# A gated linear attention with a convolution stage: exp and ln table loaded first, sine table moved between two groups of exponentials, and a new order of the whole program

## The chip, the cores and the metric

The kernel runs on one core of a Trainium2 chip. The metric is the device time of one execution in microseconds (us); lower is better. A core has five engines with a queue each that works strictly in its order: PE (TensorE, matrix products; its weight loads are listed as PEld), DVE (VectorE), ACT (ScalarE), POOL (GpSimd) and SP (SyncE, which here only issues DMAs). They wait for one another through semaphores.

## The reference

Two stages, float32 in and out: a recurrent attention (4 batches, 8 heads, 768 steps, 48 columns) and a gate with a circular convolution over the 768 steps.

```
for t in range(S):                      # state: (B, H, D, D)
    cur   = outer(u * k_t, v_t)
    y_t   = r_t @ (state + cur)
    state = w_t * state + outer(k_t, v_t)

x    = y as (B, S, H*D)
proj = x @ w_proj                       # split into x1, x2, x3
conv = irfft(rfft(x2, axis=1) * rfft(filter_fft, axis=0))
out  = (x1 * conv * x3) @ w_out
```

## The kernel before

The sequence is cut into 24 chunks of 128 steps, six to a batch. The matrices of the Fourier transform (the tiles F and mi) are made on the chip: DVE and POOL compute angles (`ang`, `ia`), ACT takes their sine (`sin0` to `sin2` and `is`, line 1520). Sine needs one table of ACT, exp and ln need another. `trig` (line 1514) loads the first, `table` (line 1564) the second; a copy works under either.

First stage, for chunk i (loads and some steps are for a group gi: chunk 0, chunk 1, then pairs):

- SP loads w, k, r, v (`lw`, `lk`, `lr`, `lv`, line 1307, 192 KB each) into rings of 3 (w) and 4 groups.
- ACT: `ln` of w (line 1313). PE: `cs`, running sums of the logarithms by a triangular mask (lines 1341 to 1344). ACT: `ex`, their exponentials in PSUM (line 1347), and `ph`, the decay of a whole chunk (line 1354). DVE: `kq`, exponentials times k and r (line 1350).
- PE: `tr`, eight transposes of kq (line 1362); `qk` copies them out of PSUM (DVE or ACT); PE: `sc`, the scores (line 1374); `mt` and `mc` copy and mask them.
- POOL and DVE: `rk`, `ru`, `rh`, `cc`, `vb`, `vc`, the term with u. PE: `ki`, `kv`, and DVE `su` (line 1425), the state handed from chunk to chunk; PE: `yi`, `ys`, `y`, the output; `xn` copies it out, `yt` (PE) and `xT` transpose it.

Second stage, for batch b: PE products `xw` (line 1653), `p` and `q` (line 1616), the forward transform `f` (line 1505), the inverse `E` (line 1708), the output `o` (line 1772); between them copies (`cxw`, `cp`, `cq`, `cf`, `cE`, `co`), sums and products on DVE and POOL (`sd`, `u`, `p`, `aE`, `dE`, `yE`), and `so`, the stores (SP, line 1788). The filter's spectrum is made once: `filt` (load), `fsd`, `h`, `hc`, `hg`. `if0` to `if3` make mirrored parts of mi. `warm n b` issues n products of zeros on PE (line 1253) that no result needs.

All of this stands as a table of operations (`plan.op`) with what they read and write. The text ORDER, some thousand lines, gives the order: the queue of an engine is its operations in the order of that text. A line names the operation, its engine (P, A, D, G for POOL, S; a few further letters choose a form: M and N mask a whole chunk's scores on DVE or ACT, C masks them on POOL in one piece, Q is an inverse with folded halves at fewer columns, V and X ways to do `xn`, "-" nothing), for PE its PSUM bank, and at times another operation on DVE that a POOL operation is to wait for.

Of the kernel before, what the change touches and what calls it, by code (L numbers as in the profile page):

```python
# [215 lines left out]
yi3 P 0
ys3 P
y3 P
tr5 P 2
xn3 D  # L220
xa3 -
qk4 A
qk5 D
yt2 P 5
rk3 G
ru3 G
lr6 S
lr7 S
lk7 S
yt3 P 1  # L230
sc4 P 3
ph5 A
xT2 A
xw0.0 P 6
lk6 S
filt S
vb3 G xn3
mt4.0 D
mt4.1 D
xT3 A  # L240
xw0.2 P 1
if0 A
cxw0.2 A
mc4.0 -
mc4.1 -
sc5 P 3
# [41 lines left out]
lv7 S
xw0.4 P 2
kq7 D  # L290
cxw0.4 A
ph7 A
p0.0.1 P 0
kq6 D
ph6 A
cp0.0.1 A
sd0.0.0 D
p0.2.1 P 2
tr6 P 4
tr7 P 5  # L300
qk6 A
cp0.2.1 D
qk7 A
# [228 lines left out]
qk12 D
xT11 A
sc12 P 6
qk13 A
aE0.0.0 D
aE0.0.1 D
cE0.1 D
mt12.1 -
lv16 S  # L540
kv12 P 3
mt12.0 N
E0.2 Q 4
su12 D
ki13 P 3
kv13 P
sc13 P 6
lv17 S
dE0.0.0 -
lr17 S  # L550
aE0.1.0 D
aE0.1.1 D
lw19 S
lk19 S
su13 D
cE0.2 A
ln8 A
p1.0.1 P 0
dE0.0.1 -
aE0.2.0 D  # L560
aE0.2.1 D
dE0.1.0 -
mt13.0 M
cs14 P 2
mt13.1 -
cp1.0.1 A
cc7 D
xw1.4 P 4
ex14 A
cxw1.4 A  # L570
vb8 A
p1.2.1 P 7
q1.0.1 P 0
kq14 D
ru8 G aE0.1.0
rh8 G mt13.0
# [1294 lines left out]
```

## Time and profile before

| what | value |
|---|---|
| median of 3 runs | 155.47 us (155.39 to 160.37) |
| the profiled execution's own time | 154.99 us |
| its span | 153.3 us |
| busy: PE, DVE, ACT, POOL | 143.9, 138.8, 123.8, 94.5 us |
| warm-up products on PE | 109, with 16.0 us of the busy time |
| granted clock of TensorE | 0.996 |
| DMA moved | 26.23 MB, mean 171 GB/s |

The profile is of one execution. A row of its timeline gives start, duration, engine, line, operation, output and inputs, count, and in square brackets the idle time before it and what ended it. A window's row gives the busy time of each engine in a stretch of the span, the clock granted to PE, the busy share of the 16 DMA engines and the rate. PE's products are pipelined, so a row's duration is longer than the distance to the next.

### The profile page before, as it was taken

The numbers are of one execution on the slowest core, as the hardware profiler recorded it, in microseconds if no ns is written. First come the engines' busy times: TensorE is split into PE (matmuls) and PEld (weight loads), VectorE is DVE, ScalarE is ACT, GpSimd is POOL, SyncE is SP. The second block draws the span as 40 slices with busy tenths as digits, with TensorE's granted clock in tenths as the row PEclk, the third lists the DMA queues.
The fourth block names the chain that finished last, engine by engine and source line by source line (L and its number), as shares of the span: only waits on it lengthen the run. The fifth ranks groups of instructions, "written<-read, shape, count | busy, mean of one in ns | idle before, by whom it ended". The sixth has DMA issues, their size and how long they took to land.

```text
span 153.3 us, 4449 instructions
## 1 busy us (share of the span) xinstructions
PE 143.9 (94%) x1742; PEld 97.3 (63%) x1742; DVE 138.8 (91%) x259; ACT 123.8 (81%) x207; POOL 94.5 (62%) x97
## 2 busy tenths in 40 slices
PE   7989899999999999999999979999999999999980
PEld 5867676576657666666566747566676666755640
DVE  7959998987989999999999899989999999999950
ACT  5699997628989978898899969999999866876370
POOL 6827979734056564889867928896889540820310
PEclk9999999999999999999999999999999999999998
DMA  5999899999989999999899899998900000002956
GB/s 99 200 227 223 166 222 172 214 182 286 230 168 212 185 184 205 181 207 216 165 213 227 162 219 186 192 209 164 361 36 0 4 0 0 4 0 82 397 208 240
DMA packets 104118, 26.23 MB, mean 171 GB/s; under 512 B 100129, under 2 KB 102690, under 8 KB 104098
## 3 DMA queue, kind: packets, MB, share of 16 engines
q1 hardware_dynamic: 102498, 24.78, 73.6%
q0 software_dynamic: 1600, 1.18, 5.6%
q8 instruction: 13, 0.21, 0.6%
q14 instruction: 7, 0.06, 0.2%
HBM read 22.41 MB, written 4.72 MB: 177 GB/s over the span
## 4 chain that ended last, share of the span: by engine, by line
PE 55%; DVE 18%; ACT 11%; issue 6%; DMA 6%; POOL 1%; ACTq 1%; SPq 0%; DVEq 0%
PE banks L1505 10%; PE banks L1616 9%; PE banks L1653 7%; PE banks L1772 6%; PE banks L1708 5%; DVE kq L1350 5%; PE banks L1362 3%; DMA w<-in_w_dram 3%; ACT banks L1347 3%; PE banks L1374 3%; DMA out_dram<-o 2%; PE banks L1253 2%; ACT lg L1313 2%; PE banks L1452 2%; DVE U L1203 2%
## 5 line engine op out<-in xcount | busy, mean ns | idle before, releaser
L1616 PE MATMUL banks<-xT,wproj 128*128 128x384 bf16 x144 | 27.6, 326 | 0.1
L1203 POOL TENSOR_TENSOR rk<-kr 128x768 bf16<-128x768 f32 (+1 forms) x13 | 22.0, 1694 | 7.8 <-DVE xT L1209 3.7
L1350 DVE TENSOR_TENSOR kq<-banks,kr 128x768 bf16<-128x768 f32 x24 | 22.5, 949 | 2.2 <-ACT banks L1347 2.0
L1207 ACT ACTIVATE x<-banks 128x768 bf16<-128x768 f32 (+1 forms) x26 | 17.8, 706 | 6.1 <-PE banks L1616 4.0
L1395 POOL TENSOR_SCALAR_AFFINE_SELECT mt<-mt 128x512 bf16<-128x512 bf16 (+1 forms) x17 | 14.4, 853 | 10.0 <-DVE rk L1323 6.0
L1203 POOL TENSOR_TENSOR vc<-vb,cc 128x768 bf16<-128x768 bf16 x11 | 17.9, 1625 | 3.6 <-DVE cc L1326 2.2
L1347 ACT ACTIVATE banks<-banks 128x768 f32<-128x768 f32 x24 | 19.3, 809 | 0.5 <-PE banks L1344 0.4
L1616 PEld LDWEIGHTS <-wproj 128*128 128x128 bf16 x144 | 13.2, 97 | 8.0 <-issue 0.4
L1207 ACT ACTIVATE qk<-banks 128x1024 bf16<-128x1024 bf16 x17 | 17.4, 1028 | 0.4 <-PE banks L1362 0.3
L1390 DVE TENSOR_TENSOR mt<-banks,mask_excl 128x1024 bf16<-128x1024 f32 (+1 forms) x18 | 16.9, 950 | 0.7 <-PE banks L1452 0.6
L1253 PE MATMUL banks<-wt 128*128 128x256 bf16 x109 | 16.0, 300 | 1.1 <-DVE wt L1276 1.1
L1362 PE MATMUL banks<-ident,kq 128*128 128x128 bf16 x192 | 14.2, 219 | 0.6 <-DVE kq L1350 0.5
L1653 PE MATMUL banks<-wproj,xT 128*128 128x384 bf16 x72 | 13.5, 326 | 1.1 <-DVE xn L1464 1.1
L1505 PE MATMUL banks<-sd,F 128*128 128x384 bf16 (+1 forms) x96 | 13.4, 328 | 0.0
L1772 PE MATMUL banks<-wout,y 128*128 128x384 bf16 x72 | 13.3, 326 | 0.0
L1253 PEld LDWEIGHTS <-wt 128*128 128x128 bf16 x109 | 10.8, 107 | 4.0 <-DVE wt L1276 1.1
L1362 PEld LDWEIGHTS <-kq 128*128 128x128 bf16 x192 | 11.3, 97 | 2.1 <-DVE kq L1350 1.5
L1207 ACT ACTIVATE o<-banks 128x768 f32<-128x768 f32 (+1 forms) x13 | 9.8, 764 | 3.5 <-PE banks L1772 3.3
L1505 PEld LDWEIGHTS <-F 128*128 128x128 bf16 (+1 forms) x120 | 8.4, 103 | 5.9 <-issue 1.5
L1641 DVE TENSOR_TENSOR g<-banks,x 128x768 bf16<-128x768 f32 (+1 forms) x16 | 11.8, 751 | 0.0
L1313 ACT ACTIVATE lg<-w 128x768 bf16<-128x768 f32 (+1 forms) x13 | 10.3, 803 | 1.6 <-DMA w<-in_w_dram 1.5
L1207 ACT ACTIVATE mt<-banks 128x512 bf16<-128x512 f32 (+1 forms) x17 | 11.5, 704 | 0.0
(109 smaller groups left out, 331.7 us busy)
## 6 DMA issues: line engine op xcount, KB each, us to landing
w<-in_w_dram SPq DMA_DIRECT2D x24, 192.0 KB, 4.4
kr<-in_r_dram SPq DMA_DIRECT2D x24, 192.0 KB, 3.8
kr<-in_k_dram SPq DMA_DIRECT2D x24, 192.0 KB, 3.9
v<-in_v_dram SPq DMA_DIRECT2D x24, 192.0 KB, 3.8
out_dram<-o SPq DMA_DIRECT2D x11, 384.0 KB, 3.5
U<-in_moe_filter_fft_dram SPq DMA_DIRECT2D x1, 1152.0 KB, 7.8
wproj<-in_moe_w_proj_dram POOLq DMA_DIRECT2D x3, 288.0 KB, 5.2
out_dram<-o SPq DMA_DIRECT2D x2, 192.0 KB, 2.2
```

What stands on the lines that cost most here:

```text
L1203: return eng(e).tensor_mul(o, a, b)
L1207: return nc.scalar.activation(out=o, in_=a, func=AF.Copy)
L1253: nc.tensor.matmul(banks[:, at, 0:256], wt[:, 0:L], wt, start=True, stop=True)
L1347: op(f"ex{i}", [ACT], lambda e, bk: nc.scalar.activation(out=two(bk, f"cs{i}")[:, :, 0:C], in_=two(bk, f"cs{i}")[:, :, 0:C], func=AF.Exp), ...
L1350: op(f"kq{i}", [DVE], lambda e, bk: nc.vector.tensor_mul(kq[f][:, :, :, 0:D], two(bk, f"cs{i}")[:, :, 0:C].rearrange("p a (h d) -> p a h d ...
L1362: nc.tensor.transpose(p[:, HP * m + j, :], kq[f][:, m, 2 * j:2 * j + 2, :], ident)
L1390: return copy(ACT, o, x) if e in (ACT, ACT2) else nc.vector.tensor_mul(o, x, _mid(mask_excl, z - HP * a))
L1395: return nc.gpsimd.affine_select(out=o, in_=o, pattern=[[0, z - HP * a], [1, L]], compare_op=ALU.is_gt, fill=0.0, base=0, channel_multipli ...
L1505: nc.tensor.matmul(p[rows], F[:, ti, c0 + rows.start:c0 + rows.stop], x[q][:, ti, :], start=(ti == 0), stop=(ti == NT - 1),)
L1616: nc.tensor.matmul(p, wproj[:, cb, col0:col0 + L], xT[bx][:, cb, sl], start=(cb == 0), stop=(cb == CB - 1),)
L1653: nc.tensor.matmul(view(bk)[:, z], xT[bx][:, cb, (c0 + z) * L:(c0 + z + 1) * L], wproj[:, cb, C:2 * C], start=(cb == 0), stop=(cb == CB - 1),)
L1772: nc.tensor.matmul(view(bk)[:, z], yt_[:, z, :], wout[:, cb, :], start=(cb == 0), stop=(cb == CB - 1),)
```

## The change

The code changes in the keys that tables stand for. A third load, `first`, brings the exp and ln table in ahead of everything on ACT. `trig` and the sines now come after the exponentials of chunks 4 and 5, then `table` brings exp and ln back for `ln4` and the exponentials of chunks 6 and 7 (`ex7`, `ex6`). ORDER is another text throughout. The operations are the same but for what follows: one more table load; 90 warm-up products for 109 (16 at the start for 46); one inverse, E0.2, in the full form for the folded one, and for it two `dE` fewer; the output of chunk 18 begins with `yi` on PE; and many copies, masks and small products on another engine than before (`ur` and `ub` from DVE to ACT, `cxw0.0`, `cxw0.2`, `cp0.0.0` and `cp0.2.0` all on DVE, three of six `ia` from DVE to POOL, `mt` in whole pieces 16 times for 13 on ACT and DVE, among others).

The code:

```diff
@@ op "ur"
-    op("ur", [DVE, ACT], lambda e, bk: copy(e, u_r, u_f), r=["uf", "trig"], w=["ur"])
+    op("ur", [DVE, ACT], lambda e, bk: copy(e, u_r, u_f), r=["uf", "first"], w=["ur"])
@@ group
-           r=keys("w", sw) + ["table", "pads"], w=[f"lg.{f}"])
+           r=keys("w", sw) + ["exp", "pads"], w=[f"lg.{f}"])
-            e, vb[fv][:, 0:n], vl[sl][:, 0:n]), r=keys("v", sl) + ["trig"], w=[f"vb.{fv}"])
+            e, vb[fv][:, 0:n], vl[sl][:, 0:n]), r=keys("v", sl) + ["first"], w=[f"vb.{fv}"])
@@ first
-           w=[f"ex.{i}"], uses=[f"cs{i}"])
+           r=["exp"], w=[f"ex.{i}"], uses=[f"cs{i}"])
-           r=[f"kq.{f}"], w=[f"phi.{f}"], uses=[f"cs{i}"])
+           r=[f"kq.{f}", "exp"], w=[f"phi.{f}"], uses=[f"cs{i}"])
@@ early
+        op("first", [ACT], lambda e, bk: nc.scalar.preload_act_table_set("natural_log_exp_and_others"),
+           w=["first", "exp"])
-        op("trig", [ACT], lambda e, bk: nc.scalar.preload_act_table_set("trig_and_small"), w=["trig"])
+        op("trig", [ACT], lambda e, bk: nc.scalar.preload_act_table_set("trig_and_small"), w=["exp", "trig"])
         op("table", [ACT], lambda e, bk: nc.scalar.preload_act_table_set("natural_log_exp_and_others"),
-           r=[f"F.{ti}" for ti in range(NT)] + ["m0"], w=["table"])
+           w=["exp", "trig"])
```

Parts of ORDER, four stretches with lines left out between them:

```diff
-wz D
-warm 46 7
-lw2 S
-zeros D
-kz0 D
-kz2 D
-smalls D
-kz3 D
-lr0 S
-maps G
-imaps G kz3
-lk0 S
-ang1 D
-ang2 D
-ia0.0 G ang2
-ia0.1 G ang2
-kz1 G
-lw0 S
-ang0 D
-ia2.0 D
-ia2.1 D
-ia1.0 D
-ia1.1 D
-maskn G
-maske G
-maski G
-rk0 G ia1.1
-pads D
-lw1 S
-trig A
-sin1 A
-sin2 A
-sin0 A
-is A
-u S
-ur D
-signs D
-table A
-ln0 A
-lw3 S
-lr3 S
-um P 4
-warm 11 7
-ub D
-ru0 D
-rh0 G ub
-cc0 D
-ln2 A
-lk3 S
-lr1 S
-lk1 S
-lr2 S
-lk2 S
-cs0 P 3
-ex0 A
-ln1 A
-kq0 D
-cs3 P 6
-lv0 S
-warm 7 0
-cs1 P 1
-ex3 A
-ph0 A
-kq3 D
-lv1 S
-lw4 S
-lv2 S
-lw5 S
-ex1 A
-kq1 D
-tr0 P 0
-cs2 P 3
-qk0 A
+wz D
+warm 16 0
+pads D
+smalls D
+zeros D
+lw0 S
+first A
+ln0 A
+imaps G
+maske G smalls
+maps G smalls
+ang2 D
+ang1 D
+lw3 S
+lw2 S
+lr0 S
+lk0 S
+kz2 G
+maskn G
+cs0 P 4
+kz0 G
+ln2 A
+u S
+signs D
+maski G
+ia1.0 G
+ex0 A
+kq0 D
+ia2.0 D
+warm 9 1
+cs3 P 6
+kz3 G zeros
+cs2 P 2
+ur A
+warm 5 1
+um P 0
+rk0 G
+ub A
+lv0 S
+lw1 S
+lr3 S
+lk1 S
+tr0 P 1
+qk0 D
+ph0 A
+vb0 A
+ex3 A
+ln1 A
+ang0 D
+ru0 G ia2.0
+rh0 G kq0
+cc0 D
+kz1 D
+vc0 D
+warm 6 0
+sc0 P 0
+warm 2 4
+cs1 P 4
+mt0.1 -
+mt0.0 N
...
-ex4 A
-mc3.0 G
-lw6 S
-su2 D
-yt1 P 3
-ki3 P 2
-wproj0 G cc2
-kq4 D
-xT1 D
-kv3 P
-ph4 A
-ex5 A
-mc2.0 -
-warm 2 5
-yi2 P 4
-ys2 P
-if1 A
-tr4 P 3
-y2 P
-xn2 A
-su3 D
-kq5 D
-xa2 -
-yi3 P 0
-ys3 P
-y3 P
-tr5 P 2
-xn3 D
-xa3 -
-qk4 A
-qk5 D
-yt2 P 5
-rk3 G
-ru3 G
-lr6 S
-lr7 S
-lk7 S
-yt3 P 1
-sc4 P 3
-ph5 A
-xT2 A
-xw0.0 P 6
-lk6 S
-filt S
-vb3 G xn3
-mt4.0 D
-mt4.1 D
-xT3 A
-xw0.2 P 1
-if0 A
-cxw0.2 A
+ex4 A
+cs5 P 2
+xa1 -
+mc2.0 -
+yt1 P 1
+su2 D
+ki3 P 0
+kv3 P
+yi2 P 6
+ys2 P
+y2 P
+mc3.1 -
+xT1 A
+kq4 D
+tr4 P 1
+ex5 A
+ph4 A
+wproj0 G su2
+kq5 D
+su3 D
+xn2 A
+yi3 P 4
+ys3 P
+qk4 A
+y3 P
+rk3 G
+xn3 D
+warm 4 6
+tr5 P 6
+qk5 D
+xa2 -
+ph5 A
+yt2 P 2
+lw7 S
+xa3 -
+yt3 P 7
+xT3 D
+xT2 D
+ki4 P 5
+warm 4 1
+sc5 P 6
+trig A
+sin0 A
+sin2 A
+vb3 G xn3
+mt5.1 -
+mc5.1 -
+ia1.1 G xT2
+kv4 P
+sc4 P 3
+ia0.1 G xT2
+mt4.0 N
+ru3 D
+rh3 D
+cc3 D
+vc3 G cc3
+warm 7 1
+xw0.2 P 0
+is A
+mt5.0 M
+su4 D
+mt4.1 -
+xw0.0 P 2
+mc5.0 -
+mc4.0 C
+yi5 P 6
+cxw0.2 D
+yi4 P 4
+cxw0.0 D
+lk7 S
+sin1 A
+table A
+ln4 A
+lr7 S
+mc4.1 -
+ys5 P
+ys4 P
+y5 P
+xn5 D
+y4 P
+xn4 D
+p0.0.0 P 0
+lk6 S
+xa4 -
+xa5 -
+yt5 P 6
+p0.2.0 P 3
+lr6 S
+rk4 G xn5
+xT5 D
+yt4 P 2
+cs7 P 6
+cp0.0.0 D
+filt S
+cp0.2.0 D
+cs6 P 4
+xT4 A
+xw0.4 P 0
+ex7 A
+kq7 D
+lv7 S
+ex6 A
+kq6 D
+cxw0.4 A
+if3 A
+p0.0.1 P 2
+tr7 P 1
+ph7 A
+cp0.0.1 A
+tr6 P 6
+qk6 A
+qk7 A
+sd0.0.0 D
+ru4 D
+lw8 S
+lw9 S
+p0.2.1 P 0
+ph6 A
...
-yi14 - 4
-ys14 P
-y14 P
-qk16 D
-xn13 A
-mc15.1 -
-xa13 -
-yt13 P 2
-xT12 A
-dE0.2.1 D
-ki16 P 3
-kv16 P
-sc16 P 6
-xn14 V
-ex17 A
-kq17 D
-xT13 A
-xw2.0 P 4
+yi14 - 3
+ys14 P
+lr18 S
+lv18 S
+yt12 P 5
+xa13 -
+su15 D
+yt13 P 2
+xT12 A
+y14 P
+xn14 X
+mc15.1 -
+ki16 P 7
+kv16 P
+sc16 P 5
+lv19 S
+lr19 S
+ln10 A
+rk9 G mt15.1
+xT13 D
+kq17 D
+mc15.0 -
+ph17 A
+mt16.1 A
+dE0.2.0 -
+xa14 G
+xw2.0 P 3
...
-lv23 S
-q2.2.1 P 7
-su20 D
-cs22 P 4
-yi18 - 2
-ex22 A
-rh11 G kq21
-sd2.1.0 D
-cq2.2.1 D
-tr21 P 6
-y18 P
-ki21 P 7
-lr22 S
-q2.0.1 P 0
-xn18 X
-sd2.0.0 D
-mc20.0 G mt20.1
-cs23 P 2
-qk21 A
-mc19.0 G
-kv21 P
-xa18 G cq2.2.1
-kq22 D
-so0.0 S
+lr22 S
+sc19 P 4
+xT16 A
+rk11 G
+lv23 S
+cs21 P 0
+xT17 A
+mt19.1 -
+mc18.1 -
+lr23 S
+so0.1 S
+xw2.4 P 2
+qk20 A
+u01.0 D
+ru11 D
+ex21 A
+p2.0.1 P 6
+vb11 G u01.0
+mt19.0 M
+p2.2.1 P 4
+kq21 D
+cxw2.4 A
+cp2.0.1 A
+ki20 P 5
+o0.2 P 2
+rh11 G
+cp2.2.1 D
+ln12 A
+kv20 P
+ph21 A
+sc20 P 0
+q2.2.1 P 4
+co0.2 A
+p1.0 D
+sd2.0.0 D
+su20 D
+mc18.0 G
+mt20.1 A
+mc20.1 G cp2.2.1
+cq2.2.1 D
+mt20.0 A
+cs22 P 6
+yi18 P 2
+y18 P
+sd2.1.0 D
+tr21 P 5
+ki21 P 4
+q2.0.1 P 0
+ex22 A
+xn18 A
+cs23 P 2
+qk21 A
+kq22 D
+kv21 P
+ph22 A
+yi19 - 6
+cq2.0.1 D
+mc19.1 -
+lk23 S
+rk12 G sd2.1.0
+so0.0 S
+su21 D
+cc11 D
+ex23 A
+xa18 -
+mc20.0 G cq2.0.1
+mc19.0 -
+kq23 D
+ys19 P
+so0.2 S
+yt18 P 5
+xT18 A
+y19 P
+E1.2 Q 0
+vc11 G
+xn19 X
+cE1.2 A
+aE1.2.1 D
+aE1.2.0 D
+E1.0 Q 4
+xa19 G
+dE1.2.1 G cc11
+ph23 A
+cE1.0 A
+aE1.0.1 D
+aE1.0.0 D
+tr22 P 6
+E1.1 Q 2
+lv22 S
+qk22 A
+cE1.1 A
+aE1.1.0 D
+aE1.1.1 D
+yi20 - 0
+ys20 P
+tr23 P 7
+y20 P
+ki22 P 6
+f2.0 P 4
+vb12 A
+kv22 P
```

More of the change, by code (lines that the diff above doesn't have):

```diff
@@ L216 @@
[L216 to L246 removed]
+lw5 S
+tr1 P 0
+rk1 G
+ru1 D
+rh1 G ru1
+ph1 A
+qk3 D
+xa0 -
+ph3 A
+kq2 D
+lv2 S
+lv3 S
+yt0 P 6
+sc3 P 4
+xT0 A
+mt3.0 M
+qk1 A
+vb1 A
+ph2 A
+warm 4 7
+tr2 P 6
+lr4 S
+lk4 S
+ki1 P 1
+sc1 P 2
+qk2 A
+mc3.0 -
+mt1.1 -
+kv1 P
+warm 2 7
+sc2 P 6
+cc1 D
@@ new lines @@
+rk2 G
+lk5 S
+ru2 D
+ia2.1 G
+vc1 G
+mc1.1 -
+mt1.0 M
+mc1.0 -
+mt2.1 -
+mt3.1 -
+lr5 S
+ln3 A
+warm 5 0
+cs4 P 4
+yi1 P 2
+rh2 G ru2
+su1 D
+vb2 G ru2
+ys1 P
+mc2.1 -
+lv5 S
+lv4 S
+cc2 D
+vc2 G cc2
+mt2.0 M
+wproj1 G mt2.0
+ki2 P 0
+y1 P
+lw6 S
+warm 5 1
+kv2 P
+xn1 A
+ex4 A
[25 more added lines that the diff above has]
+xn3 D
+warm 4 6
+tr5 P 6
@@ L288 @@
[L288 to L303, printed above, removed]
+cp0.2.1 A
+cf0.0 A
 sd0.1.0 D
-ru4 D
-f0.0 P 6
+f0.2 P 5
+sc7 P 0
+mt7.1 -
+rh4 D
 fsd0 D
@@ L532 @@
[L532 to L576, printed above, removed]
+E0.0 P 4
+mc11.0 C mt10.0
+ph12 A
+yi11 - 1
+cE0.0 A
+su10 D
@@ new lines @@
+kq13 D
+ph13 A
+tr12 P 3
+ys11 P
+kv12 P 0
+aE0.0.0 D
+rk7 G
+ru7 G
+xa10 -
+qk12 A
+y11 P
+E0.1 P 6
+xn11 V
+xa11 -
+su12 D
+cE0.1 A
+aE0.0.1 D
+dE0.0.0 -
+rh7 G aE0.0.0
+yt11 P 1
+xT11 D
+yt10 P 0
+ki13 P 3
+tr13 P 2
+E0.2 P 4
+kv13 P
+aE0.1.1 D
+aE0.1.0 D
+xT10 A
+qk13 D
+ln8 A
+cE0.2 A
+sc12 P 6
+lk18 S
+lr16 S
+mt12.1 -
+su13 D
+aE0.2.1 D
+aE0.2.0 D
+mt12.0 N
+sc13 P 0
+p1.0.1 P 2
+mt13.1 D
+mt13.0 D
+lv16 S
+cp1.0.1 A
+cs14 P 6
+ex14 A
+dE0.1.0 -
+xw1.4 P 4
+q1.0.1 P 1
+cc7 D
+kq14 D
+cq1.0.1 D
@@ L919 @@
+yi23 - 4
+p3.0.0 P 2
+yt21 P 7
 xT21 A
```

1051 lines of the change are left out of this document (439 added, 612 removed).

## Prediction

> **What bounds the kernel now.** First the page's busy shares, then windows of the span, then the timeline of the opening.
>
> ```profile
> PE 143.9 (94%) x1742; PEld 97.3 (63%) x1742; DVE 138.8 (91%) x259; ACT 123.8 (81%) x207; POOL 94.5 (62%) x97
> ```
>
> ```profile
> 0.00:5.00 5.00, 3.88 (x19) 2.76 (x20) 3.83 (x24) 3.16 (x4) 3.31 (x17) 1.00 0.66 131
> 5.00:10.00 5.00, 4.94 (x41) 3.86 (x40) 4.48 (x18) 3.74 (x4) 2.85 (x8) 1.00 1.02 202
> 10.00:15.00 5.00, 4.27 (x54) 3.29 (x54) 3.54 (x5) 5.00 (x9) 3.04 (x4) 1.00 1.14 226
> 15.00:20.00 5.00, 4.50 (x80) 3.15 (x77) 4.99 (x8) 4.51 (x11) 4.90 (x5) 1.00 0.95 184
> 20.00:25.00 5.00, 4.64 (x82) 3.26 (x77) 4.35 (x9) 3.98 (x8) 3.91 (x5) 1.00 1.05 176
> ...
> 50.00:60.00 10.00, 9.78 (x145) 6.78 (x144) 9.76 (x16) 8.02 (x14) 5.67 (x5) 1.00 1.05 186
> ...
> 100.00:110.00 10.00, 9.94 (x131) 6.67 (x130) 9.17 (x15) 9.91 (x18) 8.45 (x7) 1.00 1.00 228
> ...
> 130.00:140.00 10.00, 10.00 (x74) 6.21 (x73) 9.91 (x23) 7.12 (x13) 4.64 (x5) 1.00 0.01 2
> ```
>
> PE does real work without a break from about 30 us to the end. Up to 25 us it does not, and there the loads set the pace: the DMA engines are fully busy from 5 us on, at 226 GB/s at best, and stay so to 110 us. So the kernel has a stretch paced by loads and behind it one paced by PE.
>
> ```profile
> 0.80 1.28 ACT L1514 ACT_TABLE_LOAD   x1 [0.80 <-PEq L1855]
> ...
> 3.04 2.80 ACT L1520 ACTIVATE F<-o,mpi 128x768 bf16<-128x768 uint16 x3 [0.96 <-DVE o L1494]
> ...
> 7.07 1.25 ACT L1520 ACTIVATE mi<-U,mpi 128x1152 bf16<-128x1152 uint16 x1 [1.23 <-DVE U L1529]
> ...
> 8.34 1.28 ACT L1564 ACT_TABLE_LOAD   x1
> ...
> 9.64 1.26 ACT L1313 ACTIVATE lg<-w 128x384 bf16<-128x384 f32 x2
> ...
> 10.81 0.80 ACT L1347 ACTIVATE banks<-banks 128x768 f32<-128x768 f32 x1
> ...
> 11.64 0.96 DVE L1350 TENSOR_TENSOR kq<-banks,kr 128x768 bf16<-128x768 f32 x1 [0.79 <-ACT banks L1347]
> ...
> 15.20 0.96 DVE L1350 TENSOR_TENSOR kq<-banks,kr 128x768 bf16<-128x768 f32 x1
> ```
>
> The first exponential (10.81) waits for two tables, three sines of F, the sine of mi and two logarithms on ACT. The first kq starts at 11.64, chunk 2's at 15.20. This is what the change goes at. The second table stands between the sine that ends at 8.32 and the logarithm at 9.64: a switch took 1.28 us here, with nothing around it.
>
> ```profile
> 25.17 0.96 DVE L1350 TENSOR_TENSOR kq<-banks,kr 128x768 bf16<-128x768 f32 x1 [0.41 <-ACT banks L1347]
> ...
> 29.57 0.81 ACT L1207 ACTIVATE x<-banks 128x768 bf16<-128x768 f32 x1 [1.18 <-PE banks L1653]
> ...
> 31.35 0.84 ACT L1313 ACTIVATE lg<-w 128x768 bf16<-128x768 f32 x1 [0.98 <-DMA w<-in_w_dram]
> ...
> 35.10 0.49 ACT L1207 ACTIVATE x<-banks 128x384 bf16<-128x384 f32 x1 [2.90 <-PE banks L1616]
> ...
> 35.88 1.50 ACT L1347 ACTIVATE banks<-banks 128x768 f32<-128x768 f32 x2
> ...
> 36.71 1.82 DVE L1350 TENSOR_TENSOR kq<-banks,kr 128x768 bf16<-128x768 f32 x2 [0.65 <-ACT banks L1347]
> ```
>
> Here the change puts its sines. In 28 to 36 us ACT waits 1.18, 0.98 and 2.90 us, so there is room; but kq of chunks 7 and 6 (36.71) follows at once on the exponentials at 35.88.
>
> ```profile
> 75.41 0.32 PE L1341 MATMUL banks<-lg,mask_neg 128*128 128x384 bf16 x1 [0.24 <-ACT lg L1313]
> ...
> 90.01 1.14 PE L1653 MATMUL banks<-wproj,xT 128*128 128x384 bf16 x6 [1.12 <-DVE xn L1464]
> ```
>
> Of PE's later waits these are the largest that the timeline names.
>
> **The change part by part.** All of it is set against the profiled execution: span 153.3, own time 154.99, which is 0.48 under the median of 155.47.
>
> *First chunk.* Landings are the issue in SP's timeline plus the time to landing that the view of line 1307 gives for that one issue. w0 is now the first load; the first load of before landed 2.6 us after its issue at 0.81, so w0 is there at 3.4. The table load (0.80 to 2.08) is hidden by that wait. ln0 takes 0.51. The mask for `cs0` is made on POOL, now behind `imaps`, `maske`, `maps` and `kz2` (1.25, 0.28, 1.0, 0.3 by their rows): about 4.35. So `cs0` runs at 4.4 instead of 10.21. `ex0` stands behind `ln2`, which needs the third load (landed at 1.92 + 3.6 = 5.5): 5.5 + 0.86 + 0.81 = 7.2. k0 is the fifth load; the fifth landed at 3.7 + 3.9 = 7.6. So kq0 starts at 7.6, 4.0 us earlier.
>
> *What is left of that.* Loads before and after stand in nearly the same places of SP's queue, and SP waits for no buffer there. kq2 needs r2, now the 14th issue (the 13th landed at 13.95, the 15th at 16.8; about 15.5) against 15.20 before: no gain, and v0, moved from 14th to 7th place past six loads, is what puts them back. Chunk 5's last load is the 23rd in both: 19.96 + 4.1 = 24.1, with kq5 at 25.17 before: 1.1 us at most. Chunk 6's last is the 31st in both: 31.0 + 4.8 = 35.8, against 36.71: 0.9 at most. The early start is used up by the loads.
>
> *The sines on ACT.* After kq5 (24.1 to 25.05) ACT has qk4, ph5 and xT2 to do: 26.2. Then trig 1.28, two sines of 0.93, the mask copy of chunk 4 1.04, the sine of mi 1.25, the third sine 0.93, table 1.28, ln4 0.85: 8.5 us, to 34.7. Then `cs7` (0.45 on PE) and `ex7` at 35.25, against 35.88. What hides the 8.5 is the 5.1 us of waiting seen above and 2.5 us of copies and flips moved elsewhere. The cover is thin: from 0.6 us of delay on, each tenth moves kq7. DVE: kq7 36.05, kq6 to 37.95; PE ends tr7 and tr6 at 38.4 instead of 39.7, but three products of `p0.2.1` (0.49) now come after them: 0.8 won. Then DVE does sd 0.75, ru 0.55, sd 0.75, rh 0.47 and fsd 2.6: 43.1, against 43.34. The spectrum `h` (3.06 on PE) ends at 46.2, against 46.77 where `cs8` starts: **0.5 won**. Bounds: 0.9 won (the load) and 2.6 lost (below).
>
> [...]
>
> *PE's work.* From the distances between rows (cs 0.43, tr 0.45, sc 0.33, three 384-column products 0.49, f 1.0, E 0.98 whole and 0.65 folded) PE's order holds 123.4 us of real work before and 123.9 after: E0.2 whole 0.33, yi of chunk 18 0.17. PE is the pace there: **0.5 lost**. From 46.77 to the last product at 148.6 PE has 96.7 us to do in 101.8: 5.1 us of waiting, the most that any order can win there.
>
> *Named waits.* xw2.0 waited 1.12 us at 90.01 for its bank, which `xn14` on DVE (89.42 to 89.98) had to empty. xn14 is now on ACT behind xT12. Between 0 and 1.1: I take **0.6 won**. cs14 waited at 75.41 for ln8, which waited for w14: its place, counted in 192 KB loads, goes from 68th to 66th, about 2 us sooner at 1.06 us each. Visible 0.24, with the last product's tail 0.4: **0.3 won**.
>
> *Nothing counted.* 30 fewer warm-ups at the start and 19 fewer in all: they lay beside waits for loads. PE ran 5 to 7 of them per us up to 5.0 us, 10 to 12 afterwards; should the thinner filling keep it at the lower pace, the cover is the loads, and 15 us of work to 25 us would become at most 21 with a late bound of 1 us lost. Engine swaps by their rows: DVE 3.2 less in the opening (angles, memsets), 1.5 more after; ACT 1.4 less; POOL 0.9 more: spread over 100 us, 0, with 1 us either way.
>
> Sum: 154.99 - 0.5 + 0.5 - 0.6 - 0.3 = 154.1; with the 0.48 to the median 154.6.
>
> **Rivals.**
>
> A: the early start goes through. In 15 to 25 us the DMA moved only 184 and 176 GB/s against 226 before. Were the new order to feed it at 226, some 2.0 us of loading (10 us x 20%) go; and were half of PE's 5.1 us of later waiting to go instead of 0.9, 1.6 more: 154.6 - 3.6 = 151.0. For it: PE has 7.5 us of idle time before tr6 (38.6 less 20.7 of real work and 10.4 of warm-ups). Against: SP waited for no buffer then and the busy share was 0.95 and 1.05, so the slower rate is not SP's.
>
> B: the block on ACT is longer than its cover. Were a switch to take another 1.28 us each for emptying the engine, twice, ex7 comes at 37.9, tr6 at 41.0, and as DVE and PE take their orders strictly, all of it goes to the end: 154.6 + 2.6 = 157.2; with kq5 1.5 late as well 158.7. Against: the first switch showed nothing of it.
>
> C, the other side: the last v load stands behind stores. SP now issues so0.1, lk23, so0.0, so0.2 and only then lv22; before, all loads were out at 105.7. so0.2 waits for co0.2, whose product comes at 83.7 us of PE's real work, which is 109.0 if time runs 25.3 ahead of work as it did at kv22 before (115.3 and 90.0); behind ln12 and ph21 on ACT co0.2 ends at 110.9. lv22 issues at about 111, lands (3.8 us median, 7.0 at most) at 115 to 118; vb12 0.85; PE comes to kv22 at 117.9. So it decides from a landing at 117.0 on, and each us beyond stops PE with everything queued behind kv22 (sc21, sc22, f2.1). With ACT 3 us late, busy 9.9 of 10 us there, and the longest landing, the stop is 4.5: 159.1.
>
> **How the numbers follow.** Forecast 0.56, A 0.20, B 0.12, C 0.12. A measurement of this kernel tells about 2% from no change: 152.4 and 158.6. Faster: A and a little of the forecast's edge, 0.22. Slower: most of C, some of B, and an edge for swaps that go wrong, 0.15. Same: 0.63. The range reaches from A to C, 151.0 to 159.1; the forecast's own is 153.0 to 156.2.
>
> **What would show it.** The first exponential near 6.4 us and kq0 near 7.6, but kq2 not before 15 and kq5 not before 24; `ex7` at 35.3, kq7 at 36.0; the spectrum's last product near 46.2; no wait of over 1 us at xw2.0; PE's warm-ups 3 us less. B: an idle stretch beside the table loads near 26 and 33 us. C: PE waiting at kv22 for ACT's copy of v. A: the rate between 15 and 25 us at 220 GB/s. I am wrong if the pair 6 and 7 has its kq before 35 us, or PE waits more than 6 us after 47.

## The result, and the profile after

The changed kernel takes 154.56 us (median of 20 executions, 152.8 to 159.01); the kernel before took 155.91 us beside it (20 executions). The ratio is 0.9888, 95% interval [0.9857, 0.9918]: 1.1% less time, within the 2% that count as no change. The profiled execution took 153.79 us with a span of 152.1 us, against 154.99 and 153.3 before. Some executions take longer (the changed kernel's longest, 159.01 us, had a mean granted clock of 0.973, its shortest, 152.8, one of 1.000); medians are over all executions, ratios over the others alone, so that the medians do not divide out to the ratio.

The page of the changed kernel, busy time by engine (answers to the first line shown of before):

```profile
PE 142.4 (94%) x1725; PEld 95.3 (63%) x1725; DVE 135.6 (89%) x252; ACT 123.1 (81%) x204; POOL 96.1 (63%) x101
```

Windows of the span, changed kernel (columns as before; the last three are PE's granted clock, DMA share and GB/s):

```profile
10.00:15.00 5.00, 3.36 (x51) 2.51 (x51) 4.69 (x11) 3.56 (x7) 3.71 (x5) 1.00 1.08 215
15.00:20.00 5.00, 4.76 (x71) 3.19 (x68) 4.81 (x7) 3.53 (x6) 4.70 (x5) 1.00 0.92 179
20.00:25.00 5.00, 4.77 (x98) 3.63 (x96) 3.58 (x5) 3.81 (x7) 4.57 (x6) 1.00 1.13 212
```

Over the three windows the loads ran at 202 GB/s, against 195 before (226, 184 and 176): the new order fed the DMA engines hardly better.

ACT's timeline, changed kernel:

```profile
0.79 1.28 ACT L1517 ACT_TABLE_LOAD   x1 [0.79 <-PEq L1863]
3.52 0.52 ACT L1319 ACTIVATE lg<-w 128x384 bf16<-128x384 f32 x1 [1.45 <-DMA w<-in_w_dram]
...
6.31 0.79 ACT L1353 ACTIVATE banks<-banks 128x768 f32<-128x768 f32 x1
...
25.50 1.28 ACT L1522 ACT_TABLE_LOAD   x1
26.80 1.76 ACT L1528 ACTIVATE F<-o,mpi 128x768 bf16<-128x768 uint16 x2
...
31.69 1.28 ACT L1572 ACT_TABLE_LOAD   x1
32.98 0.84 ACT L1319 ACTIVATE lg<-w 128x768 bf16<-128x768 f32 x1
...
34.72 1.50 ACT L1353 ACTIVATE banks<-banks 128x768 f32<-128x768 f32 x2
```

The first exponential starts at 6.31 instead of 10.81. The sines stand between 25.50 and 32.97, and each of the two table loads there has only 0.01 to 0.02 us to its neighbours.

DVE's timeline, changed kernel; the rows of line 1356 are kq of chunks 0, 3 and 1, 2, 5, 7 and 6:

```profile
7.68 0.96 DVE L1356 TENSOR_TENSOR kq<-banks,kr 128x768 bf16<-128x768 f32 x1 [1.68 <-DMA kr<-in_k_dram]
...
11.85 0.56 DVE L1209 TENSOR_TENSOR vc<-vb,cc 128x384 bf16<-128x384 bf16 x1
...
12.59 1.81 DVE L1356 TENSOR_TENSOR kq<-banks,kr 128x768 bf16<-128x768 f32 x2
...
15.69 0.95 DVE L1356 TENSOR_TENSOR kq<-banks,kr 128x768 bf16<-128x768 f32 x1
...
24.32 0.96 DVE L1356 TENSOR_TENSOR kq<-banks,kr 128x768 bf16<-128x768 f32 x1 [1.29 <-DMA kr<-in_r_dram]
...
35.55 1.82 DVE L1356 TENSOR_TENSOR kq<-banks,kr 128x768 bf16<-128x768 f32 x2 [0.20 <-ACT banks L1353]
```

kq of chunk 0 is 3.96 us earlier. The pair 3 and 1 is 0.18 earlier (12.77 before), chunk 2 is 0.49 later (15.20), chunk 5 is 0.85 earlier (25.17) after 1.29 us of waiting for its load of r, and the pair 7 and 6 is 1.16 earlier (36.71).

PE's timeline, changed kernel: ahead of the filter's spectrum (24 products of line 1511), and three of the later stops that it names:

```profile
42.53 0.83 PE L1259 MATMUL banks<-wt 128*128 128x256 bf16 x6
43.29 3.22 PE L1511 MATMUL banks<-P,F 128*64 128x384 bf16 x24
...
78.36 0.65 PE L1624 MATMUL banks<-xT,wproj 128*128 128x384 bf16 x3 [0.25 <-ACT x L1213]
...
96.82 1.14 PE L1780 MATMUL banks<-wout,y 128*128 128x384 bf16 x6 [0.32 <-DVE g L1649]
...
145.15 2.61 PE L1780 MATMUL banks<-wout,y 128*128 128x384 bf16 x15 [0.18 <-POOL y L1209]
```

The spectrum starts at 43.29 against 43.71, the last products at 145.15 against 146.30. So in this pair of profiles 0.42 of the 1.15 us come from the opening and 0.73 from the time between. There the named stops fell from 2.01 us (0.22, 0.24, 0.27, 1.12, 0.16) to 0.75: 1.26 less, and about 0.5 of it went to the more work that the prediction had counted. (The last row of before holds 16 products and starts one product, 0.16 us, sooner in the work than the 15 of the changed kernel; by the ends of the two rows it is 1.30 and 0.88.) The second part of the split is not firm: the same changed kernel, run again (e0 below), took 102.65 us from the spectrum to the last products, no less than the 102.59 of before.

Two marks carry the rest of the study: kq of the pair 7 and 6, and the start of the spectrum. The profiles, one execution each, in us (e2 aside, which computed something else):

| kernel | kq0 | kq3 | kq5 | kq7 | spectrum | last products | from spectrum to last | ratio to before on its chip |
|---|---|---|---|---|---|---|---|---|
| before | 11.64 | 12.77 | 25.17 | 36.71 | 43.71 | 146.30 | 102.59 | 1 |
| changed | 7.68 | 12.59 | 24.32 | 35.55 | 43.29 | 145.15 | 101.86 | 0.9888 |
| e1, sines first | 11.28 | 16.87 | 27.39 | 38.38 | 46.12 | 149.06 | 102.94 | 0.9972 (chip 6) |
| e0, changed again | 7.49 | 12.42 | 25.84 | 38.34 | 46.09 | 148.74 | 102.65 | 0.9978 (chip 1) |
| e5, two more loads | 7.64 | 12.49 | 26.11 | 40.56 | 49.90 | 150.65 | 100.75 | 1.0118 (chip 1) |
| e6, none before spectrum | 7.92 | 13.07 | 26.45 | 38.31 | 45.86 | 148.26 | 102.40 | 0.9961 (chip 1) |
| e2b, tables alone | 11.81 | 12.93 | 25.66 | 45.48 | 52.47 | 155.97 | 103.50 | 1.0485 (chip 1) |
| e8, xn14 on DVE | 7.44 | 12.44 | 25.56 | 39.67 | 47.41 | 149.27 | 101.86 | 0.9939 (chip 10) |
| e7, few warm-ups | 7.89 | 13.02 | 25.71 | 39.45 | 47.00 | 148.80 | 101.80 | 1.0056 (chip 10) |
| e3b, quick loads | 7.42 | 12.35 | 23.13 | 34.62 | 42.36 | 144.21 | 101.85 | 0.9685 (chip 10) |
| e3, all loads quick | 6.98 | 11.91 | 22.69 | 34.19 | 41.93 | 146.48 | 104.55 | 0.956 (chip 6) |
| e4, before, all loads quick | 10.74 | 11.87 | 23.93 | 42.05 | 49.03 | 151.21 | 102.18 | 1.0122 (chip 6) |
| e4b, before, quick loads | 10.80 | 11.93 | 24.00 | 36.51 | 43.50 | 147.00 | 103.50 | 0.9867 (chip 10) |

The column to read is the last but one: apart from e5 and e3 (which stopped for weights behind the spectrum, with a granted clock of 0.7 and 0.8 in the two slices of its page from 53.7 to 61.4 us) it lies between 101.80 and 103.50, whatever was done before the spectrum. A time lost or won there comes out at the end. It also shows how far single profiles differ: by 0.79 us between e0 and the first profile, which are of one kernel.

### The profile page after: what moved, and what is told of

Same layout as the page of the kernel before. It is cut to its first block, busy times and chain, and to the rows that moved or that the text cites. A ratio compares the mean times of both kernels' runs of the same rounds, so it can differ in the third digit from the quotient of the medians.

```text
span 152.1 us, 4409 instructions
## 1 busy us (share of the span) xinstructions
PE 142.4 (94%) x1725; PEld 95.3 (63%) x1725; DVE 135.6 (89%) x252; ACT 123.1 (81%) x204; POOL 96.1 (63%) x101
## 4 chain that ended last, share of the span: by engine, by line
PE 42%; DVE 15%; DMA 13%; SPq 10%; ACT 8%; issue 5%; POOL 4%; POOLq 1%; DVEq 0%; ACTq 0%
SPq L1313 10%; PE banks L1624 7%; PE banks L1511 6%; PE banks L1780 5%; DMA w<-in_w_dram 5%; PE banks L1661 3%; PE banks L1368 3%; PE banks L1380 3%; DMA v<-in_v_dram 3%; DMA kr<-in_r_dram 3%; DVE kq L1356 3%; PE banks L1458 3%; DMA kr<-in_k_dram 2%; ACT banks L1353 2%; PE banks L1716 2%
## 5 line engine op out<-in xcount | busy, mean ns | idle before, releaser
L1209 POOL TENSOR_TENSOR rk<-kr 128x768 bf16<-128x768 f32 (+1 forms) x13 | 23.0, 1766 | 9.5 <-DMA kr<-in_r_dram 5.9
L1209 POOL TENSOR_TENSOR vc<-vb,cc 128x768 bf16<-128x768 bf16 (+1 forms) x11 | 17.4, 1577 | 5.1 <-DVE cc L1332 3.3
L1213 ACT ACTIVATE x<-banks 128x768 bf16<-128x768 f32 (+1 forms) x24 | 16.8, 709 | 1.6 <-PE banks L1661 1.1
L1396 DVE TENSOR_TENSOR mt<-banks,mask_excl 128x1024 bf16<-128x1024 f32 (+1 forms) x17 | 16.2, 965 | 0.2 <-PE banks L1380 0.2
L1213 ACT ACTIVATE qk<-banks 128x1024 bf16<-128x1024 bf16 x16 | 16.2, 1029 | 0.0
L1259 PE MATMUL banks<-wt 128*128 128x256 bf16 x90 | 14.4, 300 | 1.1 <-DVE wt L1282 1.1
L1368 PEld LDWEIGHTS <-kq 128*128 128x128 bf16 x192 | 11.8, 97 | 4.2 <-DVE kq L1356 1.6
L1213 ACT ACTIVATE mt<-banks 128x512 bf16<-128x512 f32 (+1 forms) x15 | 11.6, 802 | 1.1 <-PE banks L1380 0.7
L1213 ACT ACTIVATE o<-banks 128x768 f32<-128x768 f32 (+1 forms) x12 | 9.3, 785 | 3.5 <-PE banks L1780 3.4
L1649 DVE TENSOR_TENSOR g<-banks,x 128x384 bf16<-128x384 f32 (+1 forms) x16 | 11.8, 748 | 0.3 <-PE banks L1624 0.2
L1209 DVE TENSOR_TENSOR U<-X,hh 128x2304 bf16<-128x2304 bf16 (+1 forms) x12 | 11.9, 1022 | 0.0
```

Of the source, the lines that this page charges most:

```text
L1209: return eng(e).tensor_mul(o, a, b)
L1213: return nc.scalar.activation(out=o, in_=a, func=AF.Copy)
L1259: nc.tensor.matmul(banks[:, at, 0:256], wt[:, 0:L], wt, start=True, stop=True)
L1368: nc.tensor.transpose(p[:, HP * m + j, :], kq[f][:, m, 2 * j:2 * j + 2, :], ident)
L1396: return copy(ACT, o, x) if e in (ACT, ACT2) else nc.vector.tensor_mul(o, x, _mid(mask_excl, z - HP * a))
```

## The experiments

**Is it the table or the order?** e1 keeps the new order and undoes the table part: trig, the sines and then the exp and ln table ahead of the first exponential, with the 46 warm-ups of before and the angles made early.

```diff
-warm 16 0
...
+warm 46 0
...
-lw0 S
-first A
-ln0 A
...
+trig A
...
+sin2 A
+sin1 A
+sin0 A
+is A
+table A
+first -
+lw0 S
+ln0 A
...
-trig A
-sin0 A
-sin2 A
...
-is A
...
-sin1 A
-table A
```

> The changed order with the table part alone undone: sine table, three sines, sine of mi and then the exp and ln table first on ACT, as before the change, with the angles made early; the loads and nearly all else keep the changed order. Theory L (loads pace the opening, the early start is used up there): kq of chunk 0 goes from 7.7 to about 11.5 us, kq of chunk 2 from 15.7 to at most 17.5, kq of chunks 4 and 5 move by less than 1 us, kq of chunk 6 stays at its load, near 36; the time stays within 0.5% of the changed kernel, 0.984 to 0.994 of the kernel before. Theory S (the start itself brings the gain): the 3.8 us of chunk 0 reach the end in part, at least 1.2 us, 1.000 of the kernel before or more.

Measured: 157.45 us against 159.26 on that chip, ratio 0.9972 [0.9918, 1.0026]. Neither theory is met: kq of chunk 5 and of the pair 7 and 6 moved by 3.07 and 2.83 us, which L forbids, and the ratio is above L's range and under S's. DVE's timeline of e1, the same two rows:

```profile
27.39 0.96 DVE L1356 TENSOR_TENSOR kq<-banks,kr 128x768 bf16<-128x768 f32 x1 [0.53 <-ACT banks L1353]
...
38.38 1.82 DVE L1356 TENSOR_TENSOR kq<-banks,kr 128x768 bf16<-128x768 f32 x2 [0.20 <-ACT banks L1353]
```

Neither waits for a load, so in this order a late start goes through the engines to the spectrum, 2.83 us behind the changed kernel's first profile. The sines at their new place cost next to nothing: from kq5 to kq7 it is 11.23 us with them in between and 10.99 here without. Against the changed kernel on chip 1 (e0, below) the spectrum is only 0.03 us later, and the ratio cannot be told from e0's, nor from 1; its interval just touches that of the first result. No changed kernel was run on e1's chip, and e1's order was made for the early start. What the table part is worth at the end is therefore not shown: the ratios read 0.8% against the first result and nothing against e0.

e2 was to be the other half: the old order, with the exp and ln table first and the sines in the place of the change. As built, the load of the filter stood ahead of the sine of mi, and the two share a tile: mi was made of the filter's data, and that sine waited 7.97 us for its transfer. The run, ratio 1.0892 [1.0818, 1.0966], says nothing of the question.

> The kernel before with the table part alone done: exp and ln table first, sine table, sines and the two flips that stood between moved behind the transposes of chunks 2 and 3 on ACT, then the exp and ln table again; everything else in the order of before. Theory L: kq of chunk 0 at about 9 us (its w is still the fourth load), kq of chunk 5 still at 24.5 to 25.5; the block of 6.6 us on ACT meets 5.1 us of waiting there, so the exponentials of chunk 7 come 1 to 2 us later than 35.9; the time is 1.000 to 1.012 of the kernel before, no gain. Theory S: the gain of the change is there, 0.985 to 0.993.

e2b puts that sine ahead of the filter's load:

```diff
-filt S
...
+trig A
+is A
+filt S
+sin1 A
+sin2 A
+sin0 A
+table A
+if1 A
```

> The kernel before with the table part alone done: exp and ln table first, then behind the transposes of chunks 2 and 3 on ACT the sine table, the sines (the one of mi first, with the filter's load held behind it, as both share a tile), the exp and ln table and two flips; all else in the order of before. Theory O (the table part pays only in an order made for it): kq of chunk 0 at about 9 us, kq of chunk 5 at 24 to 25.5, but the block of 6.6 us stands on ACT in front of a copy that PE waits for, the exponentials of chunk 7 come 1 to 3 us later than 35.9, and the time is 1.003 to 1.020 of the kernel before. Theory S (the early start alone brings the gain): 0.985 to 0.993.

Measured: 164.76 us against 158.14, ratio 1.0485 [1.0442, 1.0529], far worse than either expectation. PE's timeline of e2b:

```profile
36.59 0.32 PE L1422 MATMUL banks<-S,ident 128*128 128x192 bf16 x1 [5.58 <-ACT x L1208]
```

ACT, held by 6.4 us of loads and sines in one piece and 1.0 us of flips, empties the projection's banks too late; PE stops for 5.58 us, its granted clock is 0.69 between 30 and 40 us, and kq7 comes at 45.48. kq0 gains nothing (11.81). ln0 waits 4.41 us for w0, which is late in the old order of loads, but it is done at 7.01; what holds `cs0` then is PE's own queue, where 46 and 11 warm-ups of the old order stand ahead of it:

```profile
9.16 1.38 PE L1254 MATMUL banks<-wt 128*128 128x256 bf16 x11
10.38 0.33 PE L1342 MATMUL banks<-lg,mask_neg 128*128 128x384 bf16 x1
```

Done in this way the tables' move loses in the old order; another place of the block there was not tried.

**The changed kernel on another chip.** e0 is the changed kernel with no edit.

> The changed kernel once more, as the measure for the runs beside it on the same chip: 0.986 to 0.992 of the kernel before, kq of chunk 7 at 35 to 36.5 us.

Measured: 156.94 us against 158.14, ratio 0.9978 [0.9943, 1.0014]; the interval does not meet that of the first result. DVE's timeline of e0, kq of chunk 5 and of the pair 7 and 6:

```profile
25.84 0.96 DVE L1356 TENSOR_TENSOR kq<-banks,kr 128x768 bf16<-128x768 f32 x1 [2.41 <-DMA kr<-in_r_dram]
...
38.34 1.82 DVE L1356 TENSOR_TENSOR kq<-banks,kr 128x768 bf16<-128x768 f32 x2 [0.20 <-ACT banks L1353]
```

The load of r that kq5 waits for lands 1.5 us later than in the first profile; in 10 to 15 and 20 to 25 us the DMA moved 197 and 192 GB/s instead of 215 and 212. kq7 is 2.8 us later, and so is the spectrum. The rest of the 2.8 is another load: POOL's copy of v for chunks 4 and 5 (`vb3`) waits 1.92 us for it, and PE, whose next products need the copy, stops. POOL's and PE's timelines of e0:

```profile
29.62 0.82 POOL L1215 CAST vb<-v 128x768 bf16<-128x768 f32 x1 [1.92 <-DMA v<-in_v_dram]
30.49 0.31 PE L1421 MATMUL banks<-vb,kq 128*64 128x48 bf16 x8 [1.52 <-POOL vb L1215]
```

The first profile has no such stop. e5 and e6 on the same chip and e8 on chip 10 have it too (1.03, 0.58 and 1.43 us), each behind that load. So loads that land later cost the changed kernel 2.8 us up to the spectrum. That this is why the gain shrank is likely but not shown, as the kernel before has no profile on chip 1.

**Is it the loads?** In e3 (changed kernel) and e4 (before) every load reads runs of 1536 bytes instead of 192:

```diff
-out=t[:, q], in_=x[b, :, rw, :].rearrange("h t d -> t h d"))
+out=t[:, q], in_=x[b].rearrange("h t d -> (h t d)")[(ci + q) * L * C:(ci + q + 1) * L * C].rearrange("(t h d) -> t h d", h=H, d=D))
```

> The changed kernel with w, k, r and v read as one contiguous stretch per chunk, 1536 bytes to a partition in place of eight pieces of 192 bytes: the same bytes and the same number of loads, but other elements, so it computes the recurrence of other data. Theory L: the rate in the opening goes over 226 GB/s, kq of chunk 5 comes before 21 us, kq of chunk 6 before 32, and the end 2 to 5 us sooner than the changed kernel: 0.955 to 0.977 of the kernel before. Theory S (the loads are not the pace of the opening): kq of chunk 5 within 1 us of before, end within 1 us of the changed kernel, 0.983 to 0.995.

> The kernel before with the same contiguous loads (other elements, so the recurrence of other data). Theory L: here the start on ACT becomes the pace, so it gains less than the changed kernel does from the same loads: 0.975 to 0.995 of the kernel before, and the distance between the two kernels grows from 1.1% to 2% or more. Theory S: both gain the same, the distance stays at 1.1%.

Measured: e3 152.17 us, ratio 0.956 [0.9496, 0.9624]; e4 161.25 us, ratio 1.0122 [1.0052, 1.0192]. e3's ratio is in L's range, but kq5 (22.69) and kq7 (34.19) missed its marks; e4 was slower with quicker loads, which neither theory had. PE's timeline of e4 shows the stop:

```profile
29.80 4.00 PE L1653 MATMUL banks<-wproj,xT 128*128 128x384 bf16 x12 [3.57 <-DMA wproj<-in_moe_w_proj_dram]
```

The projection's weights, which POOL's queue fetches beside the loads, took 9.4 us to land (median of three) instead of 5.2, and the granted clock was 0.78 between 25 and 30 us and 0.77 between 30 and 40; e3 stopped 2.16 us for the last of the three too, which took 9.2. So the pair tests two things at once. e3b and e4b make only the loads of chunks 0 to 5 quick, for the same comparison without that:

```diff
-out=t[:, q], in_=x[b, :, rw, :].rearrange("h t d -> t h d"))
+out=t[:, q], in_=(x[b].rearrange("h t d -> (h t d)")[(ci + q) * L * C:(ci + q + 1) * L * C].rearrange("(t h d) -> t h d", h=H, d=D) if i0 < 6 else x[b, :, rw, :].rearrange("h t d -> t h d")))
```

> The changed kernel in which only the loads of chunks 0 to 5 read whole runs of 1536 bytes instead of 192 (so those chunks are made of other rows of the inputs; instructions and sizes are the same). Theory L (loads pace the opening up to pair 6 and 7): kq2 by 15, kq5 by 23, kq7 by 34.5 instead of 35.5, and the ratio 0.004 to 0.012 below the changed kernel's. Rival O (the strict orders of DVE and ACT pace it): kq2 15.3 or later, kq5 at 23.5 or later, kq7 at 35 or later, ratio within 0.003. If the projection weights again come 2 us or more late and PE stops for them, the quick loads have only moved the queue, and kq7 tells nothing of L or O; kq2 still does.

> The kernel before with the same quick loads for chunks 0 to 5. Its kq0 stands behind the sines at 11.6, whatever the loads do. By L its kq5 comes at 23 to 24 instead of 25.2 and kq7 no more than 1 us earlier than 36.7, ratio 0.993 to 1.000; the changed kernel gains more from quick loads than this one does, since only there the loads are the limit before 12 us. By O both gain the same, under 0.5 us. If the projection weights come late here again (9.4 us to landing when all loads were quick), PE waits 2 to 4 us and the ratio is over 1.005.

Measured on one chip: e3b 152.81 us, ratio 0.9685 [0.9627, 0.9743]; e4b 155.45 us, ratio 0.9867 [0.9808, 0.9927]. With quick loads the change is thus worth 0.9685 / 0.9867 = 0.982, some 1.8% (the intervals do not meet); with the loads as they are, e8, which is the changed kernel but for one copy, had 0.9939 [0.9879, 0.9999] on the same chip. DVE's timeline of e3b:

```profile
12.35 1.81 DVE L1356 TENSOR_TENSOR kq<-banks,kr 128x768 bf16<-128x768 f32 x2
...
23.13 0.96 DVE L1356 TENSOR_TENSOR kq<-banks,kr 128x768 bf16<-128x768 f32 x1 [0.53 <-ACT banks L1353]
...
34.62 1.82 DVE L1356 TENSOR_TENSOR kq<-banks,kr 128x768 bf16<-128x768 f32 x2 [0.20 <-ACT banks L1353]
```

kq5 no longer waits for a load; it is 1.2 us earlier than in the changed kernel's first profile and kq7 0.9. But kq3 stands at 12.35 all the same, and chunk 2's at 15.37. Theory L (loads) holds from chunk 5 on, though kq5 and kq7 miss its marks by 0.1 us, theory O (the engines' own orders) before it. The ratio fell by more than L had: 0.020 against the first result and 0.025 against e8 on the same chip, where it had 0.004 to 0.012. e4b gained more than the 0.000 to 0.007 expected as well, and its kq0 came at 10.80, though it was to stand at 11.6 whatever the loads do.

**How thin is the cover of the sines?** e5 loads two tables more behind the last sine:

```diff
+for name in ("natural_log_exp_and_others", "trig_and_small", "natural_log_exp_and_others"):
+    got = nc.scalar.preload_act_table_set(name)
```

> The changed kernel with two table loads more at the end of the block of sines (exp and ln, sine, exp and ln): 2.57 us more on ACT if a load is 1.28 us with nothing around it. Theory T (the block's cover is thin and ACT, DVE and PE pass a delay on): kq of chunk 7 at 37.5 to 38.2, the spectrum's products 1.5 to 2.6 us later, the end 1 to 2.6 later: 0.995 to 1.006 of the kernel before. Theory A (later waits and warm-ups take it up): the end moves by less than 0.5 us, 0.986 to 0.992. [...]

Measured: 159.28 us, ratio 1.0118 [1.0061, 1.0176], 0.014 above e0 on the same chip, or 2.2 us. ACT's timeline of e5:

```profile
34.37 3.86 ACT L1574 ACT_TABLE_LOAD   x3
38.24 0.84 ACT L1319 ACTIVATE lg<-w 128x768 bf16<-128x768 f32 x1
```

Three loads take 3.86 us, 1.29 each, and the logarithm starts 0.01 us behind them. Of the 2.58 us added, kq7 shows 2.22 (40.56 against 38.34) and the last products 1.91. There is next to no cover left there. The spectrum was 3.81 late, though. PE had stopped 2.18 us for the logarithm, and the products behind the stop ran slower, at a granted clock of 0.83 between 40 and 50 us (1.00 in e0); PE's timeline of e5, and then of e0 with the same twelve products:

```profile
39.99 1.84 PE L1666 MATMUL banks<-wproj,xT 128*128 128x384 bf16 x6
41.62 2.13 PE L1629 MATMUL banks<-xT,wproj 128*128 128x384 bf16 x6
```

```profile
37.77 1.14 PE L1661 MATMUL banks<-wproj,xT 128*128 128x384 bf16 x6
38.74 1.14 PE L1624 MATMUL banks<-xT,wproj 128*128 128x384 bf16 x6
```

From the first of them to the transposes it is 3.55 us instead of 2.03, which is 1.52 of the 1.59 lost between kq7 and the spectrum. Half of the 3.81 was made up behind it: e0's named stops there sum to 1.34 us (0.48, 0.45, 0.23, 0.18) and e5 has one of 0.17. The other 0.7 is left open.

**The warm-ups.** e6 takes away the 15 in three groups before the spectrum:

```diff
-warm 4 7
...
-warm 5 7
...
-warm 6 4
```

> The changed kernel without the 15 warm-up products that stand between the transposes of chunk 6 and the filter's spectrum. In the changed kernel's trace the spectrum starts at 43.29, behind six of them, though its input was ready at 42.5. Theory W (they delay PE): the spectrum starts at 42.5 to 42.7, the end 0.4 to 0.8 us sooner: 0.983 to 0.987 of the kernel before. Theory D (the copies of the spectrum on ACT and DVE and the loads behind are the pace there): the spectrum starts sooner, the end moves by less than 0.2 us: 0.987 to 0.991. Theory C (PE's clock falls without them): the products after it take longer, 0.990 or more.

Measured: 157.1 us, ratio 0.9961 [0.9911, 1.0012] against 0.9978 for e0: not to be told apart. In its profile the spectrum then waits 0.52 us for ACT's mask copy instead of standing behind six warm-ups, and starts 0.23 us earlier than e0's. So those warm-ups mostly fill a wait, and none of the three theories stands out.

e7 takes away all but the first three groups. It was built to leave the opening alone, but in fact the 60 products are missing from about 9 us on:

```diff
-warm 6 0
...
-warm 2 4
...
-warm 4 1
```

> The changed kernel without the warm-up products behind the first 24 us; those of the opening stay. Theory Z (they lie beside waits and cost and bring nothing, as the prediction counted them): ratio within 0.003 of the changed kernel's, PE's real work starts within 0.3 us of the same times, granted clock 1.0. Rival W (some stand in the way, as the six before the spectrum that ran from 42.53 to 43.29 after its input was done at 42.51): the spectrum starts up to 0.7 us earlier and the ratio falls by 0.003 to 0.006. Rival K (they keep the clock up): a stretch between 25 and 60 us with a granted clock under 0.95 and a ratio higher by 0.005 or more.

Measured: 158.75 us, ratio 1.0056 [1.0004, 1.0108]; e8 on the same chip, with all of them, 0.9939 [0.9879, 0.9999]. Windows of e7:

```profile
10.00:15.00 5.00, 2.52 (x36) 1.89 (x37) 4.74 (x11) 3.65 (x8) 3.69 (x5) 0.70 1.02 199
15.00:20.00 5.00, 4.66 (x59) 3.59 (x57) 4.31 (x7) 3.19 (x8) 3.89 (x4) 0.61 0.96 186
```

The granted clock falls to 0.70 and 0.61, where it was 1.00 in the changed kernel, and the 16 transposes of chunks 3 and 1 take 1.86 us instead of 1.05. Expectation K named the clock, from 25 us on; there it was 0.93 up to 30 us and 0.83 up to 40, and e8's own profile has 0.83 in that last stretch too. But it is not one profile only: the mean clock of the span was 0.925 to 0.961 in all twelve executions of e7 and 0.973 to 1.000 in all twelve of e8. So taking the products away lowered the clock. That the clock is the whole of the 1.2% is the likeliest reason, not a shown one.

**The wait at xw2.0.** e8 gives xn14 back to DVE:

```diff
-xn14 X
+xn14 V
...
-xa14 G
+xa14 -
```

> The changed kernel with xn14 put back on DVE as before, in its present place of the order. The term in question: the 1.12 us that xw2.0 waited for xn14's bank in the kernel before, and 0.03 or less in the changed one. Theory N (the move of xn14 to ACT took that wait away): a wait of 0.8 to 1.3 us at xw2.0 is back, the last product of y23 ends 0.6 to 1.1 us later than in the changed kernel, and the ratio to the kernel before rises by 0.004 to 0.007 against the changed kernel's. Rival M (the rest of the new order took it away): the wait at xw2.0 stays under 0.4 us and the ratio stays within 0.003 of the changed kernel's (0.989 in its own runs, 0.998 on another chip).

Measured: 157.87 us, ratio 0.9939 [0.9879, 0.9999], between the changed kernel's two ratios. The profile has a clock of 0.80 and 0.86 between 15 and 25 us and 0.83 between 30 and 40, so only what lies behind the spectrum, at a clock of 1.00, is read from it. PE's timeline of e8:

```profile
92.24 1.14 PE L1661 MATMUL banks<-wproj,xT 128*128 128x384 bf16 x6 [0.47 <-DVE xn L1470]
```

The wait is back, with 0.47 instead of 1.12 us. But xw2.0 starts 44.83 us behind the spectrum, against 44.74 in the changed kernel, the stop at the output product (0.32) is gone in turn, and the last products come 101.86 us behind the spectrum in both. Neither theory is met: the wait is under N's 0.8 and over M's 0.4. xn14's engine accounts for 0.47 of the 1.12 us at that place; at the end nothing of it is seen, and with 0.79 us between two profiles of one kernel nothing so small could be.

## Why the prediction was right, and which of its steps were not

The forecast of 154.6 us met the median of 154.56, by two errors that cancel: its sum for the profiled execution was 154.1 against 153.79, 0.3 too much, and it put the median 0.48 above that, where it was 0.77. Luck is in it on the other side too: the kernel before, measured beside the changed one, took 155.91 and not the 155.47 that the forecast set out from. The forecast gain was 0.9 us, 0.6%; the measured one is 1.1%.

- *First chunk*: cs0 at 4.49 (4.4 forecast), ex0 at 6.31 (6.4), kq0 at 7.68 (7.6). Right.
- *"The early start is used up by the loads"*: half right. kq2 at 15.69 and kq5 at 24.32 were forecast at about 15.5 and 24.1. But 3.8 of the 4.0 us are gone at kq3 already, with no load in the way: DVE does chunk 0's own work first (the angles, cc0, vc0 at 11.85) and quick loads leave kq3 at 12.35; from kq0 to kq3 it is 4.9 us in both. kq2 came near its number by luck: DVE went on to it without waiting for r2. The loads decide from chunk 5 on, 0.9 to 1.2 us of it (e3b), 1.5 to 2.8 the other way on a chip where they come later (e0). And without the early start the new order has kq5 3.07 us later (e1): the start is needed there, not only used up. Both causes were in the profile; the step named one.
- *The sines on ACT*: kq7 35.55 against 36.05, spectrum won 0.42 against 0.5. Right at the spectrum, with kq7 0.5 us earlier than forecast and the six warm-ups ahead of the spectrum in place of that. "The cover is thin" is shown by e5: 2.58 us more, 2.22 at kq7.
- *PE's work and the named waits*: 0.73 won from the spectrum on, where the terms gave 0.4 (0.6 and 0.3 won, 0.5 lost). The sum is near, but single profiles differ by as much (0.06 lost in e0). The cause given for the largest term is right in part only: with xn14 back on DVE 0.47 of the 1.12 us at xw2.0 returned (e8). That the rest went by the other changes of the order is inferred. The reading "real work without a break from about 30 us" is too strong: 32 warm-ups of before stand between 29.8 and 47.8 us.
- *Nothing counted for fewer warm-ups*: right for the 19 that were dropped (clock 1.00 throughout the opening), though the warm-ups' busy time fell by 1.6 us (16.0 to 14.4) and not by 3. e7 shows that the next step is not free.
- *Rival A*: did not happen (195 GB/s between 15 and 25 us, against 180 before and 220 for A). Its reason was sound: with quick loads the change is worth 1.8% (e3b, e4b), with the loads as they are 0.6% on that chip (e8). The DMA engines were busy in that stretch (0.92 and 1.13). The size of the pieces moved the rate by far more (215 to 361 GB/s between 10 and 15 us, at a busy share of 1.08 and 1.04, e3b) than the order did (195 to 202 between 10 and 25 us).
- *Rival B*: refuted. No run shows the 1.28 us more at a switch: a load took 1.28 or 1.29 us, and from its end to the next activation it is 0.01 to 0.02 us in three places, at 25.50, at 31.69 and in e5 (34.37).
- *Rival C*: did not happen. The last load of v was issued at 108.24, not 111, and its copy ran at 114.99, before 117.0.

What the prediction did not reckon with is how much the pace of the loads differs between measurements (between 10 and 25 us 202 GB/s at first and 191 in e0): the same kernel won 1.1% at first and 0.2% on chip 1.

## What to carry to other kernels

Take a mark behind the disturbed stretch (here the spectrum's start) and compare kernels by the time up to it and the time from it: that tells which half a change acted in, and whether an early win lives, as far as it is larger than what two profiles of one kernel differ by (0.79 us here): profile the same kernel twice first. A first result that comes early is worth only what the next waits leave of it; ask which work fills the time it frees, and which load the next step waits for. An engine whose order is strict must be given the room first and the block of work second: the move of a table and four sines cost 4.85% in one order (e2b against before) and no loss that could be measured in another (e0 and e1, on two chips).
